# Attention slots in twos beside the mixer's channel steps, a planner with measured durations, and some weight sums on VectorE

## The chip, the core and the metric

The kernel runs on one core of one Trainium2 chip. The metric is the device time of one execution in microseconds, the median of ten runs. Every time below is of a device execution or of its profile.

## The reference

Block-sparse attention (BigBird), and after it a Fourier mixing block with a two-layer channel network. Cut to what matters:

```python
# q, k, v: (4 batches, 8 heads, 768 positions, 64), float32
scores = scale * q @ k.T                       # 768 x 768 for each head
mask: blocks of 32; the neighbours, first and last block rows and columns,
      and 3 sampled blocks for each block row
attn = exp(where(mask, scores, -1e9) - max); attn /= sum(attn)
x = (attn @ v)                                 # heads side by side: (4, 768, 512)

mixed = real(fft(fft(x, axis=1), axis=2))      # positions, then features
u = x + mixed
un = (u - mean(u)) / sqrt(var(u) + 1e-6)       # over features
out = u + relu(un @ w_ch1) @ w_ch2             # 512 -> 2048 -> 512
```

## The kernel before

**Engines.** TensorE (PE) multiplies, ScalarE (ACT) takes exponentials and copies out of the accumulation banks (PSUM), VectorE (DVE) adds, multiplies and folds, GpSimd (POOL) adds weights up, SyncE (SP) issues DMAs. Each takes its instructions strictly in the order in which the program issues them, and waits on semaphores. That order is fixed when the kernel is built: the source is a program that issues instructions slot by slot, with the framework's scheduler off.

**Attention.** Heads are taken in pairs: four pairs a batch, 16 in all, numbered n. For each pair the 768 queries are cut in two halves, and the 768 keys in six chunks of 128. One (pair, half, chunk) is a *unit*; two units are a *slot*. So there are 6 slots to a pair (s = 0 to 5 within it), 24 to a batch and 96 in all. A half takes three slots. For each slot the program issues:
- `scores`: for each unit two concurrent products, of 64 rows each, into one of the two score buffers `s` (L565). In the first batch, and in the second until its mixer steps turn to the channels, a second product adds the mask from two small factors (L575, `by_pe`).
- `weigh`: ScalarE's exponential into one of four buffers `e` (L585); where TensorE hasn't added the mask, the exponential in place (L588) and VectorE's product with the mask, `e<-s,mask` (L590). From the second batch on it also has GpSimd add the weights of a half up, unit after unit in place, in `acc` (L602, two adds a unit).
- `values`, for the slot before: two concurrent products of 64 columns into `o` (L615); after a half is complete, `o` is copied out, and later transposed into the mixer's input x (`place`, L637).
- `total` (L695): the sums over the keys from `acc`. In the first batch `add_up` (L681) does this on TensorE instead.
- `turn` (tp, L498): transposes of q and k of the next pair, in halves, through the one bank with the tag "t". From the third batch on, VectorE transposes in blocks, and ScalarE puts q in order (`in_order`, L540).

**The weights.** During the first batch, 32 chunks of the channel weights arrive by DMA in six rooms in turn, and ScalarE and VectorE round them (`w_round`, the last of five VectorE steps is L461). `keep_factors` (L478) copies the mask's two factors by two DMAs into room 2, after chunk 26 has been its last chunk, and from then on L575 reads the copy.

**The mixer.** While a batch's attention runs, the batch before goes through the mixer. Its first part stands in the queue `apart`: the scaling of rows (L723), folds of x on VectorE (`fold_0`, `fold_1`, `fold_e`, `fold_2`: L746 to L774), transforms on TensorE (zp, side, pq), arrival, normalisation on VectorE with a power on GpSimd (`spread`, L886), and transposes (utp). When it is through, its last step `go` puts the second part in the queue `late`: `quad`s (xp, yp, z: L1010, seven products each, which use both score buffers too) and channel steps y (L1066). Short steps (`place`, `total`, `turn`) wait in the queue `short`.

**The planner.** What is issued when between the slots is decided by estimates: `when` holds for each engine the time up to which it is planned to be busy, `busy(engine, us, after)` moves it on, and `free` holds when banks come free. `gap` issues a step of `apart` or `short` if its inputs and bank are planned to be ready. `state["owed"]` paces `late`, so that channel steps are spread over the slots of a batch.

The order of one slot before, as the source has it:

```python
for u, ps in scores(units): weigh(u, ps)
if not late: gap(1.5)
for u in done: values(u)          # the slot before
...                               # loads, short steps, channel steps
w_loads(); w_steps(sl)
if sl == SB - 3: keep_factors()   # SB = 24
```

Of the kernel before, what the change touches and what calls it, by code (L numbers as in the profile page):

```python
# [17 lines left out]
ALU = mybir.AluOpType  # L18
# [84 lines left out]
def kernel(  # L103
# [14 lines left out]
    nc = tc.nc  # L118
# [88 lines left out]

    pairs = [(b, j) for b in range(B) for j in range(NP)]
    loaded, v_of = {}, {}


    BY_VECTOR = 2 * NP + 1
# [269 lines left out]
    s_at, e_at, oT_at, acc_at = {}, {}, {}, {}  # L482

    def turn(n, a, half):

        t = loaded[n, a]
        if half == 0:
# [3 lines left out]
        tag, pool = ("m", ps_m) if first and a == 0 else ("t", ps_t)  # L491
        tp, at = pool.tile([P, 512], FP32, tag=tag, name="tp"), bank(tag)
        if a == 0:
            parts = [t[:, c // 2, c % 2, :, :] for c in (range(4, 6) if half else range(4))]
        else:
            parts = [t[:, T * half + c, :, :] for c in range(T)]
        for c, part in enumerate(parts):
            nc.tensor.transpose(tp[:, c * P:(c + 1) * P], part, ident)  # L498
        done = busy("PE", 0.15 * len(parts)) + HOP
        if a == 1:  # L500
            nc.scalar.copy(out=dst[:, half * HS:(half + 1) * HS], in_=tp[:, 0:HS])
            give(at, busy("ACT", 0.5, done))
        else:
            for i, (to, to_jump, frm, jump, cnt, step) in enumerate(_TURNED[half]):
                on, copy = (("DVE", nc.vector.tensor_copy) if n == 0 and half == 1
                            else ("ACT", nc.scalar.copy))
                copy(out=_grid(dst, to, 2, to_jump, cnt, 1),
                     in_=_grid(tp, frm, 2, jump, cnt, step))
                end = busy(on, 0.27 if cnt > 1 else 0.18, done)
            give(at, end)  # L510
        if half == 1:
# [67 lines left out]
    def weigh(u, s):  # L579
        n, w = divmod(u, UP)  # L580
        half, c = divmod(w, C)
        e = ep.tile([P, 2, HS], FP32, tag="e", name="e")
        e_of[u] = e
        if u in by_pe:
            nc.scalar.activation(out=e, in_=s[:, :, 0:HS], func=ACT.Exp, scale=scale)  # L585
            e_at[u] = busy("ACT", 0.8, s_at[u]) + HOP
        else:
            nc.scalar.activation(out=s[:, :, 0:HS], in_=s[:, :, 0:HS], func=ACT.Exp, scale=scale)  # L588
            m = mask[:, c, half * HS:(half + 1) * HS].rearrange("p (o s) -> p o s", o=1)
            nc.vector.tensor_tensor(out=e, in0=s[:, :, 0:HS], in1=m.broadcast_to([P, 2, HS]),  # L590
                                    op=ALU.mult)
            e_at[u] = busy("DVE", 0.97, busy("ACT", 0.8, s_at[u]) + HOP) + HOP
        if n < NP:
            return
        if c > 0:
            acc_at[n, half] = busy("POOL", 2.0, e_at[u]) + HOP
        if c == 1:
            acc_of[n, half] = acc_p.tile([P, 2, HS], FP32, tag="acc", name="acc")

        for i in range(2 if c > 0 else 0):  # L600
            acc = acc_of[n, half][:, i, :]
            nc.gpsimd.tensor_add(out=acc, in0=e_of[u - 1][:, i, :] if c == 1 else acc,  # L602
                                 in1=e[:, i, :])

    def values(u):
        n, w = divmod(u, UP)
        half, c = divmod(w, C)
        e = e_of[u]
        busy("PE", 0.75, e_at[u])
        vt = v_of[n]  # L610
        if c == 0:
            o_of[n, half] = ps_o.tile([P, HS], FP32, tag="o", name="o")
        o = o_of[n, half]
        for i in range(2):
            nc.tensor.matmul(o[D * i:D * i + D, :], vt[:, i, c, :], e[:, i, :],  # L615
                             start=(c == 0), stop=(c == C - 1))
# [118 lines left out]
    def fourier(b, xA, xB, uns):  # L735
# [163 lines left out]
                                    scalar2=rstd, op0=ALU.subtract, op1=ALU.mult)  # L899

        def d(us, fn, *args):
            return "d", lambda: fn(*args), 0.0, 0.0, us
# [302 lines left out]
    SP = UP // SLOT  # L1205
    SB = SP * NP
    W_PACE = 1.42
    short, apart, late = deque(), deque(), deque()
    state = {"w": 0, "got": 0, "owed": 0.0, "ready": 0.0}

    def channel_step():
        late.popleft()[0]()

    def do_apart():
        kind, fn, pe, act, dve, _ = apart.popleft()
        if kind in "dw":
# [12 lines left out]
        if kind != "-":  # L1229
            give(at, done - HOP)  # L1230
        state["ready"] = done

    def gap(rest=0.0, ahead=None, kinds="tm"):
# [4 lines left out]
        while apart:  # L1238
            kind, fn, pe, act, dve, need = apart[0]
            if len(late) > need:  # L1240
                break
            if kind in "dw":
# [26 lines left out]
    def begin(b):  # L1269
# [10 lines left out]
            factors["at"] = None  # L1280
        apart.append(("-", go, 0.0, 0.0, 0.0, hold))

    def w_loads():
# [9 lines left out]
    def slot(sl):  # L1293
        phase, r = divmod(sl, SB)
        n, s = divmod(sl, SP)
        units = range(SLOT * sl, SLOT * sl + SLOT)
        if sl < B * SB:
            for u, ps in scores(units):
                weigh(u, ps)
        if not late:  # L1300
            gap(1.5)
        if 0 < sl <= B * SB:
            done = [u - SLOT for u in units]
            for u in done:
                values(u)
            if phase == 0 or sl == SB:
                add_up(done)
            for u in done:
                e_of.pop(u)
        if s == 3 and n + 2 < len(pairs):  # L1310
# [5 lines left out]
        if sl > 0 and s == (5 if reuse else 3) and sl <= B * SB:  # L1316
            b, j = pairs[n]
            at = oT_at[n, 0]
            if reuse:
# [17 lines left out]
            short.append(("t", at, lambda: place(n - 1, 1)))  # L1337
        if sl > SB and s == 0 and sl <= B * SB:
            short.append(("t", acc_at[n - 1, 1], lambda: total(n - 1)))
        if n + 1 < len(pairs):  # L1340
            for at, a, half in ((1, 0, 0), (2 if n > 0 else 3, 0, 1), (4, 1, 0), (5, 1, 1)):
                if s == at and n + 1 < BY_VECTOR:
                    short.append(("t", 0.0, lambda a=a, half=half: turn(n + 1, a, half)))
            if s == 1:
                load_v(n + 1)
        if sl == 0:
# [5 lines left out]
        if r == 1 and 0 < phase:  # L1352
# [5 lines left out]
        gap(max(state["owed"], 0.0))  # L1358
        while late and state["owed"] >= late[0][1] / 2:
            state["owed"] -= late[0][1]  # L1360
            channel_step()
            gap(max(state["owed"], 0.0))

        while short and (s in (2, 5) or len(short) > 1 or phase == 0 or r == 0):
            ready = [i for i in short if max(i[1], min(free[i[0]])) <= when["PE"] + 0.1]
            if not ready and s not in (2, 5) and r > 0 and sl > 1:
                break
            item = ready[0] if ready else short[0]
            short.remove(item)
# [153 lines left out]
```

## Time and profile before

| | |
|---|---|
| median of 10 runs | 1090.04 us (1087.92 to 1092.57) |
| the profiled execution | 1087.79 us, its span 1086.1 us |
| granted TensorE clock, mean | 0.994 |
| ScalarE busy | 378.9 us, 35% of the span |
| slot 24 (second batch) begins | 129.84 us |
| slot 48 (third batch) begins | 294.06 us |
| slot 72 (fourth batch) begins | 557.16 us |
| last scores (slot 95) begin | 799.62 us |
| the chain that ended last | TensorE 90%, VectorE 5%, ScalarE 2% |
| GpSimd's adds (L602), two a unit | 192 at 1076 ns and 48 at 1061 ns on the mean |

Rows of the timeline have the start in us from the span's beginning, the time from there to the end of the group, engine, line, operation, what is written and read, the shapes, the number of instructions, and in brackets the idle time of the engine ahead of it and what ended it. Instructions of TensorE overlap, so the spacing of starts tells what they cost. A float32 product is two passes, and so two instructions in the trace (x8 of s are two units). In the rows of windows follow the stretch, its length, then busy time and instructions of TensorE, its weight loads, VectorE, ScalarE and GpSimd, then the granted clock, the DMA share and GB/s. The rows of a tile give least, median and greatest duration in ns, first and last start, and shapes.

### The profile page before, as it was taken

Reading aid. Unit: us, or ns where it says so; the run is one execution under the profiler, and the core shown is the slowest. Engines: PE = TensorE matmul, PEld = TensorE weight load, DVE = VectorE, ACT = ScalarE, POOL = GpSimd, SP = SyncE. Lnnn points to the kernel's source line nnn. Section 1 sums busy time; section 2 is a strip of 40 time slices with the busy share of each in tenths; the row PEclk is TensorE's granted clock in tenths of the full one; section 3 lists DMA queues with packets and bytes.
Section 4 is the critical chain, followed back from the end, with each engine's and each line's share of the span. In section 5 each row is a group of like instructions: output and inputs, shape, how many; then the busy total and the mean of one; then the engine's idle time right before and its main releaser. Section 6 shows DMA issues by size and latency. Waiting matters only on the chain.

```text
span 1086.1 us, 12509 instructions
## 1 busy us (share of the span) xinstructions
PE 1052.1 (97%) x4410; PEld 536.9 (49%) x4410; DVE 648.4 (60%) x1203; ACT 378.9 (35%) x762; POOL 274.1 (25%) x302
## 2 busy tenths in 40 slices
PE   8999889999999999999999999999999999999996
PEld 4434335454444555443444555443344555568575
DVE  5899783554468265665577446555557355675663
ACT  5888655552331212344342302334320202220210
POOL 1000094852343001355455000344630001000000
PEclk9999899999999999999999999999999999999998
DMA  7757311110110001223211000212000001000001
GB/s 223 219 175 238 97 31 30 44 30 15 19 25 1 1 1 33 55 40 56 43 21 32 1 0 15 64 33 40 12 8 7 1 0 30 30 1 0 1 19 44
DMA packets 108483, 47.07 MB, mean 43 GB/s; under 512 B 95854, under 2 KB 101244, under 8 KB 108412
## 3 DMA queue, kind: packets, MB, share of 16 engines
q1 hardware_dynamic: 106524, 45.38, 16.3%
q10 hardware_dynamic: 1856, 0.79, 0.3%
q8 instruction: 37, 0.61, 0.2%
q14 instruction: 34, 0.28, 0.1%
q0 software_dynamic: 32, 0.01, 0.0%
HBM read 37.11 MB, written 6.29 MB: 40 GB/s over the span
## 4 chain that ended last, share of the span: by engine, by line
PE 90%; DVE 5%; ACT 2%; issue 1%; DMA 1%; POOL 0%; SPq 0%; POOLq 0%; ACTq 0%; DVEq 0%
PE y L1066 23%; PE z L1010 15%; PE s L565 11%; PE o L615 11%; PE yp L1010 8%; PE yy L1129 6%; PE xp L1010 4%; PE zp L823 2%; PE tp L498 1%; PE sp L681 1%; PE s L575 1%; PE utp L935 1%; PE sp L695 1%; PE zp L794 1%; PE xt L637 1%
## 5 line engine op out<-in xcount | busy, mean ns | idle before, releaser
L602 POOL TENSOR_TENSOR acc<-acc,e 128x384 f32<-128x384 f32 x192 | 200.3, 1076 | 127.5 <-DVE e L590 118.0
L565 PE MATMUL s<-qT,kT 64*128 64x384 f32 x768 | 153.6, 515 | 5.2 <-DVE e L590 3.8
L615 PE MATMUL o<-e,vr 128*64 128x384 f32 x768 | 146.4, 503 | 0.0
L1069 DVE TENSOR_TENSOR x<-y,x 128x512 f32<-128x512 f32 x72 | 49.7, 690 | 147.7 <-PE y L1066 147.7
L1066 PE MATMUL y<-w_sb,hA 128*128 128x512 f32 x288 | 131.1, 598 | 1.7 <-ACT zs L825 1.7
L1066 PE MATMUL y<-w_sb,hB 128*128 128x512 f32 x288 | 129.0, 597 | 0.7 <-DVE x L1069 0.7
L590 DVE TENSOR_TENSOR e<-s,mask 128x768 f32<-128x768 f32 x106 | 96.3, 949 | 45.2 <-ACT s L588 43.0
L588 ACT ACTIVATE s<-s 128x768 f32<-128x768 f32 x106 | 80.3, 789 | 116.6 <-PE s L565 116.0
L602 POOL TENSOR_TENSOR acc<-e 128x384 f32<-128x384 f32 x48 | 49.9, 1061 | 234.7 <-ACT e L585 129.9
L565 PEld LDWEIGHTS s<-qT,kT 64*128 64x128 f32 x768 | 63.5, 185 | 80.0 <-issue 23.0
L1010 PE MATMUL z<-unT,t 128*128 128x384 f32 x256 | 93.0, 486 | 0.0
L1015 DVE TENSOR_TENSOR hA<-z,hA 128x384 f32<-128x384 f32 x64 | 35.7, 558 | 89.5 <-PE z L1010 88.7
L1066 PEld LDWEIGHTS y<-w_sb,hB 128*128 128x128 f32 x288 | 53.2, 190 | 67.6 <-issue 65.6
L1066 PEld LDWEIGHTS y<-w_sb,hA 128*128 128x128 f32 x288 | 52.4, 190 | 65.7 <-issue 58.5
L615 PEld LDWEIGHTS o<-e,vr 128*64 128x64 f32 x768 | 46.8, 137 | 74.7 <-issue 70.1
L886 POOL TENSOR_SCALAR st<-st 128x1 f32<-128x1 f32 x24 | 6.7, 279 | 280.6 <-DVE st L885 280.2
L585 ACT ACTIVATE e<-s 128x768 f32<-128x768 f32 x86 | 65.1, 813 | 27.5 <-PE s L575 26.1
L1019 ACT ACTIVATE hA<-hA 128x384 f32<-128x384 f32 x64 | 33.5, 523 | 117.8 <-DVE hA L1015 117.4
L1010 PEld LDWEIGHTS z<-unT,t 128*128 128x128 f32 x256 | 48.6, 190 | 33.9
L1019 ACT ACTIVATE hB<-hB 128x384 f32<-128x384 f32 x64 | 33.5, 523 | 86.4 <-DVE hB L1015 86.4
L1010 PE MATMUL xp<-unT,w_sb 128*128 128x384 f32 x128 | 47.7, 495 | 0.3 <-DVE x L1069 0.3
L1010 PE MATMUL yp<-unT,w_sb 128*128 128x384 f32 x128 | 46.9, 489 | 0.5 <-DVE un L859 0.5
(202 smaller groups left out, 1387.9 us busy)
## 6 DMA issues: line engine op xcount, KB each, us to landing
wraw<-in_moe_w_ch_dram SPq DMA_DIRECT2D x32, 512.0 KB
vr<-in_v_dram SPq DMA_DIRECT2D x30, 192.0 KB
qr<-in_q_dram SPq DMA_DIRECT2D x48, 64.0 KB
x<-oT SPq DMA_DIRECT2D x192, 12.0 KB
kr<-in_k_dram SPq DMA_DIRECT2D x14, 192.0 KB
qb<-in_q_dram SPq DMA_DIRECT2D x28, 96.0 KB
kb<-in_k_dram SPq DMA_DIRECT2D x28, 96.0 KB
out_dram<-x SPq DMA_DIRECT2D x16, 128.0 KB
```

Of the source, the lines that this page charges most:

```text
L565: nc.tensor.matmul(s[:, i, 0:HS], kT[rows, c * P:(c + 1) * P], qT[rows, queries], start=True, stop=u not in by_pe)
L585: nc.scalar.activation(out=e, in_=s[:, :, 0:HS], func=ACT.Exp, scale=scale)
L588: nc.scalar.activation(out=s[:, :, 0:HS], in_=s[:, :, 0:HS], func=ACT.Exp, scale=scale)
L590: nc.vector.tensor_tensor(out=e, in0=s[:, :, 0:HS], in1=m.broadcast_to([P, 2, HS]), op=ALU.mult)
L602: nc.gpsimd.tensor_add(out=acc, in0=e_of[u - 1][:, i, :] if c == 1 else acc, in1=e[:, i, :])
L615: nc.tensor.matmul(o[D * i:D * i + D, :], vt[:, i, c, :], e[:, i, :], start=(c == 0), stop=(c == C - 1))
L1010: nc.tensor.matmul(to, a[:, k, :], c[:, k, :], start=(k == 0), stop=(k == ND // 2 - 1))
L1015: tt(out=to, in0=ps, in1=a, op=ALU.add)
L1019: nc.scalar.activation(out=h, in_=h, func=ACT.Relu)
L1066: nc.tensor.matmul(y, hs[0, half][:, l, m * P:(m + 1) * P], w2_sb[:, 4 * r + l, :], start=(l == 0), stop=(l == 3))
L1069: nc.vector.tensor_tensor(out=x[:, m, :], in0=y, in1=x[:, m, :], op=ALU.add)
L1129: nc.tensor.matmul(ps, a[:, k, :], c[k // 2][:, k % 2, :] if isinstance(c, list) else c[:, k, :], start=(k == 0), stop=(k == 3))
```

## The change

1. *Slots in twos.* From the first even slot with channel steps in `late`, two slots are issued together: scores of the even slot, values of the two slots before, scores of the odd slot, and channel and short steps only after that. Where the first of the two waiting slots ends a half, its values come ahead of the even slot's scores. Values thus run up to two slots behind (the queue `due`).
2. *Planned durations.* A GpSimd sum is put down at 2.9 us instead of 2.0. A fold is planned 0.75 us longer for each of its instructions while GpSimd is planned to be busy. The planner also tracks when a buffer `e` is free again (`e_free`).
3. *Sums.* In the second batch, where TensorE adds the mask, the sum of a unit is issued after its values, and VectorE does it, in one add of 128 x 768, if it is planned to be done sooner than GpSimd would be. As built, 19 units go to VectorE, and GpSimd keeps 202 of its 240 adds.
4. *Banks and places.* From the pair n = 5 on, the second half of q is transposed through a bank with the tag "m" instead of "t". `keep_factors` runs in slot 19 instead of 21. `total` is issued by s = 1 at the latest. Loads of q, `place` and the mixer's beginning follow the new place of the values; other short steps may wait longer, and all are forced at s = 3 and 5 once slots are paired.

Cut to its core:

```diff
+    def turn_on(n, a, half):
+        return "m" if n > NP and (a, half) == (0, 1) else "t"
...
-            e_at[u] = busy("ACT", 0.8, s_at[u]) + HOP
+            e_at[u] = busy("ACT", 0.8, max(s_at[u], e_free.pop(u - 2 * SLOT, 0.0))) + HOP
...
-        if n < NP:
-            return
-        if c > 0:
-            acc_at[n, half] = busy("POOL", 2.0, e_at[u]) + HOP
...
+            if n >= NP:
+                gather(u)
+
+    def gather(u):
+        n, w = divmod(u, UP)
+        half, c = divmod(w, C)
+        if c == 0:
+            return
...
+        at = max(e_at[u], acc_at.get((n, half), 0.0))
+        if u in by_pe and factors["at"] and max(when["DVE"], at) + 1.0 < max(when["POOL"], at) + 2.9:
+            nc.vector.tensor_tensor(out=acc, in0=start, in1=e, op=ALU.add)
+            acc_at[n, half] = busy("DVE", 1.0, at) + HOP
+        else:
+            for i in range(2):
+                nc.gpsimd.tensor_add(out=acc[:, i, :], in0=start[:, i, :], in1=e[:, i, :])
+            acc_at[n, half] = busy("POOL", 2.9, at) + HOP
+        e_free[u] = acc_at[n, half]
...
+        if u in by_pe and n >= NP:        # in values(u), after its products
+            gather(u)
...
+        OPS = {fold_0: 1, fold_1: 1, fold_e: 3, fold_2: 2}
+    def behind(kind):
+        at = max(when["DVE"], state["ready"])
+        return 0.75 * (len(kind) - 1) if when["POOL"] > at else 0.0
...
-        if sl < B * SB:
-            for u, ps in scores(units):
-                weigh(u, ps)
-        if not late:
-            gap(1.5)
-        if 0 < sl <= B * SB:
-            done = [u - SLOT for u in units]
...
+        opens = sl % 2 == 0
+        state["paired"] |= opens and len(late) > 0
+        paired = state["paired"]
...
+        if paired and len(due) == 2 and due[0] % SP % T == T - 1:
+            sum_up()
+        got = scores(units) if sl < B * SB else ()
+        if paired and len(due) == 2:
+            sum_up()
+        for u, ps in got:
+            weigh(u, ps)
+        if not paired and not late:
+            gap(1.5)
+        while due and (opens or not paired):
+            sum_up()
+        due.append(sl)
...
+        more = paired and opens and sl < B * SB
+        if not more:
+            gap(rest())
+        while not more and rest():
             state["owed"] -= late[0][1]
             channel_step()
+            gap(rest())
...
-        if sl == SB - 3:
+        if sl == SB - 5:
             keep_factors()
```

`sum_up` takes the first slot of `due`, and issues `values` for its units (and in the first batch `add_up`). Nothing in the order after the last attention slot changes but that its last values come two slots at a time.

More of the change, by code (lines that the diff above doesn't have):

```diff
@@ L481 @@
     turned, e_of, acc_of, o_of, sums_of, x_of, sp_of = {}, {}, {}, {}, {}, {}, {}
-    s_at, e_at, oT_at, acc_at = {}, {}, {}, {}
+    s_at, e_at, e_free, oT_at, acc_at = {}, {}, {}, {}, {}
+    def turn_on(n, a, half):
+        return "m" if n > NP and (a, half) == (0, 1) else "t"
     def turn(n, a, half):
         t = loaded[n, a]
-        if half == 0:
+        first_of = (n, a) not in turned
+        if first_of:
             turned[n, a] = tp_p.tile([P, S], FP32, tag="qk"[a] + "T", name="qk"[a] + "T")
@@ L490, in turn @@
         first = n == 0 and half == 0
-        tag, pool = ("m", ps_m) if first and a == 0 else ("t", ps_t)
+        tag, pool = ("m", ps_m) if first and a == 0 or turn_on(n, a, half) == "m" else ("t", ps_t)
         tp, at = pool.tile([P, 512], FP32, tag=tag, name="tp"), bank(tag)
@@ L510, in turn @@
             give(at, end)
-        if half == 1:
+        if not first_of:
             flat = t.rearrange("p t r i d -> p (t r i d)" if a == 0 else "p c i d -> p (c i d)")
@@ L592, in weigh @@
             e_at[u] = busy("DVE", 0.97, busy("ACT", 0.8, s_at[u]) + HOP) + HOP
-        if n < NP:
+            if n >= NP:
[4 more added lines that the diff above has]
+        if c == 0:
             return
-        if c > 0:
-            acc_at[n, half] = busy("POOL", 2.0, e_at[u]) + HOP
         if c == 1:
             acc_of[n, half] = acc_p.tile([P, 2, HS], FP32, tag="acc", name="acc")
[L600 to L603, printed above, removed]
+        acc, e = acc_of[n, half], e_of[u]
+        start = e_of[u - 1] if c == 1 else acc
+        at = max(e_at[u], acc_at.get((n, half), 0.0))
[7 more added lines that the diff above has]
+        e_free[u] = acc_at[n, half]
     def values(u):
@@ L901, in d @@
         def d(us, fn, *args):
[L902 removed]
+            return "d" + "d" * OPS.get(fn, 0), lambda: fn(*args), 0.0, 0.0, us
+        OPS = {fold_0: 1, fold_1: 1, fold_e: 3, fold_2: 2}
         first = [d(1.8, fold_0, 0), d(1.8, fold_0, 1), d(1.0, fold_1, 0), d(0.9, fold_e),
@@ L1207 @@
     W_PACE = 1.42
-    short, apart, late = deque(), deque(), deque()
-    state = {"w": 0, "got": 0, "owed": 0.0, "ready": 0.0}
+    short, apart, late, due = deque(), deque(), deque(), deque()
+    asked = set()
+    needed = set()
+    state = {"paired": False, "total": None, "w": 0, "got": 0, "owed": 0.0, "ready": 0.0}
     def channel_step():
         late.popleft()[0]()
+    def behind(kind):
+        at = max(when["DVE"], state["ready"])
+        return 0.75 * (len(kind) - 1) if when["POOL"] > at else 0.0
     def do_apart():
         kind, fn, pe, act, dve, _ = apart.popleft()
-        if kind in "dw":
+        if kind[0] in "dw":
+            dve += behind(kind)
             state["ready"] = busy("DVE", dve, rstd_at[0] if kind == "w" else state["ready"]) + HOP
@@ L1241, in gap @@
                 break
-            if kind in "dw":
+            if kind[0] in "dw":
+                dve += behind(kind)
                 if kind == "w" and rstd_at[0] > max(when["DVE"], when["PE"]) + 0.2:
@@ L1281, in begin, with rest, once @@
         apart.append(("-", go, 0.0, 0.0, 0.0, hold))
+    def rest():
+        return state["owed"] if late and state["owed"] >= late[0][1] / 2 else 0.0
+    def once(*of):
+        if of in asked:
+            return False
+        asked.add(of)
+        return True
     def w_loads():
@@ L1296, in slot, with sum_up @@
         units = range(SLOT * sl, SLOT * sl + SLOT)
-        if sl < B * SB:
-            for u, ps in scores(units):
-                weigh(u, ps)
-        if not late:
-            gap(1.5)
-        if 0 < sl <= B * SB:
-            done = [u - SLOT for u in units]
+        opens = sl % 2 == 0
+        state["paired"] |= opens and len(late) > 0
+        paired = state["paired"]
+        def sum_up():
+            at = due.popleft()
+            done = range(SLOT * at, SLOT * at + SLOT)
             for u in done:
                 values(u)
-            if phase == 0 or sl == SB:
+            if at < SB:
                 add_up(done)
@@ L1309, in slot @@
                 e_of.pop(u)
-        if s == 3 and n + 2 < len(pairs):
+        if paired and len(due) == 2 and due[0] % SP % T == T - 1:
[10 more added lines that the diff above has]
+        due.append(sl)
+        if s >= (4 if paired else 3) and n + 2 < len(pairs) and (n + 2, 0) not in loaded:
             load_q(n + 2)
@@ L1315, in slot @@
         reuse = n % NP == 0 and phase >= 2
-        if sl > 0 and s == (5 if reuse else 3) and sl <= B * SB:
+        if s >= (5 if reuse else 3) and (n, 0) in oT_at and once(n):
             b, j = pairs[n]
@@ L1339, in slot @@
             short.append(("t", acc_at[n - 1, 1], lambda: total(n - 1)))
+            state["total"] = short[-1]
+        if r == 0:
+            needed.clear()
+            needed.update(map(id, short))
         if n + 1 < len(pairs):
-            for at, a, half in ((1, 0, 0), (2 if n > 0 else 3, 0, 1), (4, 1, 0), (5, 1, 1)):
-                if s == at and n + 1 < BY_VECTOR:
-                    short.append(("t", 0.0, lambda a=a, half=half: turn(n + 1, a, half)))
+            for at, a, half in ((1, 0, 0), (2 if n > 0 else 3, 0, 1),
+                                (3 if paired else 4, 1, 0), (5, 1, 1)):
+                if s >= at and n + 1 < BY_VECTOR and once(n + 1, a, half):
+                    short.append((turn_on(n + 1, a, half), 0.0,
+                                  lambda a=a, half=half: turn(n + 1, a, half)))
             if s == 1:
@@ L1351, in slot @@
             short.append(("m", 0.0, lambda: mask_step(sl - 4)))
-        if r == 1 and 0 < phase:
+        if r > 0 and 0 < phase and not needed.intersection(map(id, short)) and once("mixing", phase):
             begin(phase - 1)
@@ L1357, in slot @@
         state["owed"] = min(state["owed"], pace) + pace if late else 0.0
-        gap(max(state["owed"], 0.0))
-        while late and state["owed"] >= late[0][1] / 2:
+        more = paired and opens and sl < B * SB
+        if not more:
+            gap(rest())
+        while not more and rest():
             state["owed"] -= late[0][1]
             channel_step()
-            gap(max(state["owed"], 0.0))
-        while short and (s in (2, 5) or len(short) > 1 or phase == 0 or r == 0):
+            gap(rest())
+        must = (3, 5) if paired else (2, 5)
+        soon = r == 0 and all(i[1] < when["PE"] + 1.0 for i in short)
+        if s == 1 and state["total"] in short:
+            short.remove(state["total"])
+            state["total"][2]()
+        while short and (not more or soon) and (
+                s in must or len(short) > 1 or phase == 0 or soon or sl == B * SB):
             ready = [i for i in short if max(i[1], min(free[i[0]])) <= when["PE"] + 0.1]
-            if not ready and s not in (2, 5) and r > 0 and sl > 1:
+            if not ready and s not in must and 1 < sl < B * SB and not soon:
                 break
```

## The prediction

> **What bounds the kernel now.** I read four views in this order. First the page's busy times: TensorE is busy for 97% of the span, and no other engine comes near.
>
> ```profile
> PE 1052.1 (97%) x4410; PEld 536.9 (49%) x4410; DVE 648.4 (60%) x1203; ACT 378.9 (35%) x762; POOL 274.1 (25%) x302
> ```
>
> So a gain has to be TensorE's own work or one of its few waits. The second view, who waited for whom on TensorE, names them (total, times, longest):
>
> ```profile
> PE s L565 <- DVE e L590: 3.8, 3, 1.7
> PE zp L794 <- DVE sa L767: 3.7, 1, 3.7
> PE tp L498 <- ACT qT L507: 3.4, 3, 1.1
> PE s L575 <- DMA factors<-at_q: 3.3, 1, 3.3
> ```
>
> The third is the timeline, for the price of a change of array shape. Scores use 64 rows (s, L565), values 64 columns (o, L615), the mixer the whole array:
>
> ```profile
> 466.81 1.56 PE L565 MATMUL s<-qT,kT 64*128 64x384 f32 x8
> 468.30 1.51 PE L615 MATMUL o<-e,vr 128*64 128x384 f32 x8
> 469.74 1.56 PE L1010 MATMUL xp<-unT,w_sb 128*128 128x384 f32 x4
> 471.13 1.45 PE L1010 MATMUL yp<-unT,w_sb 128*128 128x384 f32 x4
> 472.42 1.45 PE L1010 MATMUL z<-t,w_sb 128*128 128x384 f32 x4
> ```
>
> Read the starts. yp to z is 1.29 us for four passes of 384 columns with no change of shape. xp, the first after o, takes 1.39; o, changed on both sides, 1.44; s 1.49. The last pass before a change costs 0.10, the first after it 0.10, or 0.05 for o. A change therefore costs 0.15 to 0.20 us.
>
> The fourth is the timeline around the moved copy of the mask factors:
>
> ```profile
> 106.69 0.49 PE L575 MATMUL s<-at_q,at_k 64*128 64x384 bf16 x4
> 110.56 0.69 DVE L461 TENSOR_TENSOR w_sb<-w_sb,wraw 128x512 f32<-128x512 f32 x1
> 111.16 3.82 SPq L252 DMA_DIRECT2D qr<-in_q_dram  x6
> 115.08 0.55 SPq L478 DMA_DIRECT2D factors<-at_k  x1
> 115.68 0.60 SPq L478 DMA_DIRECT2D factors<-at_q  x1
> 119.07 0.82 PE L575 MATMUL s<-factors 64*128 64x384 bf16 x4 [3.27 <-DMA factors<-at_q]
> ```
>
> 106.69 is the mask step of slot 20, 119.07 that of slot 22. L461 at 110.56 is the last step of weight chunk 26, the last user of the room that the factors are copied into.
>
> **Part by part**, against the profiled execution (1087.79 us, span 1086.1; the median of the runs is 2.25 higher).
>
> *Slots in twos.* s, o, channels, s, o, channels becomes s, o, o, s, channels. In the built order of TensorE's instructions shape changes go from 350 to 319. By kind most of those lost are o to full array (39), scores to o (26) and full array to scores (21); 25 o to scores and 22 scores to full array are new. 31 fewer at 0.15 to 0.20 is 4.6 to 6.2; kind by kind with the edges above, **-5.0**. All of it is on the path. Does the pair bring a wait? The second s needs the score banks that VectorE's mask product reads: from the starts at 463.66 (s), 464.62 (exp) and 465.52 (two products, 1.82) the first product ends 2.8 us after its s began. The pair gives it 1.49 + 2.71 = 4.2 us, and at the end of a half (o, s, o, s) 2.9, as back-to-back slots have now at 0.12 each. In one place only (slot 73 to 74) just 1.95 us stands between two scores: **+1.0**.
>
> *More mask products on TensorE.* The first batch's channels start three slots later, so slots 43 and 44 add their mask by matmul: two runs at 0.32, **+0.6**.
>
> *ScalarE's reordering copy (L540, 1.86).* At 461.11 and 715.37 it holds up the exponentials, and the next scores wait (1.73 each in the timeline, with edges 1.8). Paired, it is issued between the exponentials of both slots: those of the first end 2.5 us after its s, the copy then ends at 4.4, and the second slot's exponential starts at 4.2 + 0.96 = 5.2. **-3.6.**
>
> *Factors copied two slots earlier.* The order of SyncE puts the copies ahead of the six q loads, but also has slots 20 and 21 read the copy. It cannot start before chunk 26 ends, 110.56 + 0.69 = 111.25, and nothing ahead of that differs. From issue to use took 119.07 - 115.08 = 4.0 us, so slot 20's mask step can start at 115.25, not at 106.69: a wait of **8.6**. Slot 22's present wait (its scores start at 114.19, would end at 115.6, and the mask step comes at 119.07) is 3.4. Net **+5.1**; if two copies without q loads beside them land in 2 us, +3.2. Behind the wait stand o and sp of slot 19 on TensorE; slot 20's exponentials and behind these the ScalarE steps of chunks 27 and 28. The q loads move from 111.16 to about 112.5 for a use near 141. After the 3.4 us wait the clock was halved:
>
> ```profile
> 119.00:125.00 6.00, 5.93 (x24) 1.76 (x24) 3.72 (x8) 1.89 (x3) 0.00 (x0) 0.52 0.00 0
> ```
>
> PEclk is 0.52 there, and TensorE's work took 2.4 us longer. I charge the same once more: no change. [...]
>
> *Second q half in the other bank.* Where six transposes share one bank, the second two wait for ScalarE's six copies: 1.28 with edges, at 142 and 209. Both go, **-2.6**. One k pair (slot 41) now stands without an o between: ScalarE's 0.48 copy and the hops, **+0.6**.
>
> *VectorE adds weights.* 19 of the 35 sums in which TensorE adds the mask go to VectorE: one 128x768 add each, nearest row L590 (same size, from PSUM), 949 ns; 38 GpSimd adds (median about 1.0, longest 2.5) go. TensorE waits for neither, but for the folds (1st batch, from 148 us), which GpSimd's adds slow down:
>
> ```profile
> L750 DVE TENSOR_TENSOR sa<-sa x4: 949/950/1749, 152.8 to 832.2; 128x765 f32<-128x765 f32 x4
> L767 DVE TENSOR_TENSOR sa<-sa x4: 550/551/1345, 159.4 to 836.1; 128x384 f32<-128x384 f32 x4
> ```
>
> Least and greatest are the same instruction without and with GpSimd adding beside it: 0.8 us each. Now zp waits 3.7 for sa and 0.9 (with edges) for e: 4.6. Afterwards zp stands one slot later: TensorE arrives at 157.06 + 5.1 - 1.28 + 3.25 = 164.1. The row scaling ahead of the folds (6.25) loses contention in four of six (1.04 to 0.69, the row of L1069): -1.4; one add, +1.0; so folds start at 147.96 + 5.1 - 0.4 = 152.7. sa was ready 12.7 later; two of the slowed folds then run after GpSimd has finished (-1.6): 163.8. No wait for sa, none for e. But the total (sp) now stands right behind zp, and needs the add queued behind the last fold: about 0.8. So **-3.8**; with contention as now the waits are 2.6 + 1.1 + 1.9 = 5.6, that is +1.0. [...]
>
> The other adds go in order: behind an add that waits for GpSimd's previous one stand evictions of the mixer and totals. No row shows such a wait. Below, a gain is excluded: between 164 and 250 us TensorE has no wait to lose but the one at 209. Above, one GpSimd sum (two adds at 11.61 / 8 = 1.45, so 2.9) in two places makes 5.8. I take **+1.0**, near the lower end, since VectorE is busy for only 45.0 of those 86 us.
>
> Sum: -5.0 + 1.0 + 0.6 - 3.6 + 5.1 - 2.6 + 0.6 - 3.8 + 1.0 = **-6.7**. The profiled time becomes 1081.1, the median 1090.0 - 6.7 = **1083.3**.
>
> **Rivals.** *The folds stay as late as now* (contention merely changes sides): waits at zp and sp of 5.6, -6.7 + 4.8 = -1.9, 1088.1. [...] Against: GpSimd keeps only 7 of the 10 sums of the pair of heads that runs there. *VectorE's queue blocks*: its adds wait for GpSimd's in the same sum, in slots 26 to 44, and folds and whitening behind them go late. From 6.7 us of added waits on, the change is slower: two sums of 2.9 waited for (5.8) in place of my 1.0, and the waits at zp and sp kept (4.8), give -6.7 + 4.8 + 4.8 = +2.9, 1092.9. For it: VectorE takes its instructions in order, and the sums alternate between the two engines. Against: only one such add stands between the row scaling and the folds, and GpSimd's part of its sum should be done some 3 us earlier. *The copy lands early or the wait is hidden*: -1.9 more, and no add loss, 1080.4. That pairing does not happen is excluded by the order.
>
> **How the numbers follow.** Forecast 0.50, folds as late 0.22, queue blocked 0.16, copy early 0.12. A measurement here tells 0.2%, 2.2 us, from no change. Faster takes the forecast, the early copy and a third of "folds as late" (0.69), same the rest of that (0.15), slower the blocked queue (0.16). The range reaches from 1079, the early copy with changes at 0.20, to 1092, just short of the blocked queue's centre.
>
> **What would show it.** TensorE's wait for the factors should read some 8 us near 107 to 115 with the half clock behind it; tp on qT only once; s on e gone near 461; zp on sa below 1; the third of these failing means folds, an acc on VectorE waiting on GpSimd means the queue. I'm wrong if slot 24 starts less than 3 us late, or if the second scores of a pair wait over 0.5 us throughout.

## The result, and the profile after

The changed kernel takes 1083.09 us (median of 18 runs, 1082.10 to 1084.07), the kernel before 1088.05 (62 runs, 1085.07 to 1092.57): ratio 0.995, 95% interval 0.9942 to 0.9959. The kernel before thus ran 2 us faster over many runs than in the ten of the opening table. The profiled execution took 1084.00 us, span 1082.2, against 1087.79 and 1086.1: 3.8 us less. So there are two figures for the gain, 3.8 between the two profiled runs and 5.0 between the medians; experiments 1 to 4 bear on why they differ.

The page's busy times:

```profile
PE 1047.1 (97%) x4418; PEld 540.9 (50%) x4418; DVE 657.1 (61%) x1218; ACT 377.9 (35%) x762; POOL 236.5 (22%) x264
```

TensorE still bounds, with 5.0 us less busy time. VectorE has gained 15 instructions, and GpSimd lost 38. Who waited for whom on TensorE (total, times, longest):

```profile
PE s L580 <- DMA factors<-at_q: 8.8, 1, 8.8
...
PE xp L1033 <- DVE x L1092: 2.6, 3, 1.8
PE s L570 <- DVE e L595: 2.2, 2, 1.3
...
PE tp L503 <- ACT qT L512: 1.1, 1, 1.1
...
PE zp L814 <- DVE sa L787: 0.9, 1, 0.9
PE xt L657 <- DVE sums L685: 0.8, 1, 0.8
...
PE tp L503 <- ACT kT L506: 0.6, 1, 0.6
```

The wait for the factors has grown from 3.3 to 8.8. The one for sa fell from 3.7 to 0.9, and two of the three for qT are gone. The one of scores for the mask products (s on e) fell from 3.8 in three places to 2.2 in two, and neither of the two is at the old places. xp waiting for x (1.8 in one place), xt for sums and tp for kT are not among the four that were read before. The timeline around the moved copy, SP's queue and the score products:

```profile
104.99 1.56 PE L570 MATMUL s<-qT,kT 64*128 64x384 f32 x8
...
111.02 0.53 SPq L479 DMA_DIRECT2D factors<-at_k  x1
111.60 0.59 SPq L479 DMA_DIRECT2D factors<-at_q  x1
115.34 0.82 PE L580 MATMUL s<-factors 64*128 64x384 bf16 x4 [8.79 <-DMA factors<-at_q]
```

The copy starts at 111.02, where chunk 26 lets it, and is used 4.3 us later, now by slot 20, whose scores begin at 104.99 (`L580` is the mask product that stood at L575 before). The clock behind it, by windows (start:end, length, busy times of PE, PEld, DVE, ACT and POOL, granted TensorE clock, DMA share, GB/s):

```profile
108.00:114.70 6.70, 0.00 (x0) 0.00 (x0) 2.82 (x5) 0.00 (x0) 0.00 (x0) 0.69 0.66 214
114.70:121.00 6.30, 5.66 (x24) 1.63 (x26) 0.00 (x0) 1.55 (x3) 0.00 (x0) 0.52 0.00 2
```

It is halved during the wait already, and TensorE works at half clock until 120.7. The row scaling ahead of the folds in the first batch (least, median, greatest ns; first and last start), and the chain behind it up to zp and the total (sp):

```profile
L743 DVE TENSOR_TENSOR x<-x,r x6: 679/681/1480, 146.7 to 150.6; 128x512 f32<-128x512 f32 x6
```
```profile
152.10 2.55 DVE L766 TENSOR_TENSOR sa<-x 128x1536 f32<-128x1536 f32 x1
...
155.46 9.09 POOL L619 TENSOR_TENSOR acc<-acc,e 128x384 f32<-128x384 f32 x6
157.04 1.75 DVE L770 TENSOR_TENSOR sa<-sa 128x765 f32<-128x765 f32 x1
...
163.62 1.35 DVE L787 TENSOR_TENSOR sa<-sa 128x384 f32<-128x384 f32 x1
165.00 0.56 DVE L788 TENSOR_TENSOR sa<-sa 128x384 f32<-128x384 f32 x1
165.02 0.94 PEld L814 LDWEIGHTS zp<-cs_sb,sa 128*128 128x128 f32 x4 [1.32 <-DVE sa L787]
...
167.13 0.95 DVE L614 TENSOR_TENSOR acc<-acc,e 128x768 f32<-128x768 f32 x1
168.14 0.14 PEld L715 LDWEIGHTS sp<-acc,pick 128*32 128x32 f32 x4 [0.83 <-DVE acc L614]
```

Four of the six scalings run at 680 ns, without GpSimd beside them. The folds run beside GpSimd as before, up to and with the first of L787 (1.35 against 0.55); only what comes after 164.55, where GpSimd's adds end, is undisturbed. The total then waits 0.83 for VectorE's add of weights (L614) that is queued behind the folds.

### The profile page after: what moved, and what is told of

Read it like the earlier page. It is cut to its first block, busy times and chain, and to the rows that moved or that the text cites. A ratio compares the mean times of both kernels' runs of the same rounds, so it can differ in the third digit from the quotient of the medians.

```text
span 1082.2 us, 12497 instructions
## 1 busy us (share of the span) xinstructions
PE 1047.1 (97%) x4418; PEld 540.9 (50%) x4418; DVE 657.1 (61%) x1218; ACT 377.9 (35%) x762; POOL 236.5 (22%) x264
## 4 chain that ended last, share of the span: by engine, by line
PE 90%; DVE 6%; ACT 1%; issue 1%; DMA 0%; POOL 0%; SPq 0%; ACTq 0%; POOLq 0%; DVEq 0%
PE y L1089 23%; PE z L1033 15%; PE s L570 12%; PE o L633 11%; PE yp L1033 8%; PE yy L1152 6%; PE xp L1033 4%; PE zp L843 2%; PE sp L701 1%; PE tp L503 1%; PE s L580 1%; PE zp L814 1%; PE utp L958 1%; PE sp L715 1%; PE xt L657 1%
## 5 line engine op out<-in xcount | busy, mean ns | idle before, releaser
L619 POOL TENSOR_TENSOR acc<-acc,e 128x384 f32<-128x384 f32 x162 | 165.6, 1058 | 232.4 <-ACT e L590 142.4
L633 PE MATMUL o<-e,vr 128*64 128x384 f32 x768 | 142.6, 500 | 0.0
L595 DVE TENSOR_TENSOR e<-s,mask 128x768 f32<-128x768 f32 x102 | 92.8, 951 | 56.6 <-ACT s L593 49.3
L593 ACT ACTIVATE s<-s 128x768 f32<-128x768 f32 x102 | 77.5, 792 | 98.3 <-PE s L570 97.9
L590 ACT ACTIVATE e<-s 128x768 f32<-128x768 f32 x90 | 68.5, 816 | 39.4 <-PE s L580 33.8
L619 POOL TENSOR_TENSOR acc<-e 128x384 f32<-128x384 f32 x40 | 44.9, 1142 | 109.6 <-PE sp L715 92.5
```

What stands on the lines that cost most here:

```text
L619: nc.gpsimd.tensor_add(out=acc[:, i, :], in0=start[:, i, :], in1=e[:, i, :])
```

## The experiments

They ran on three chips, each beside the kernel before, and ratios are to that; its median was 1087.01 (experiments 1, 2, 6 and 7), 1089.2 (4, 5, 8 and 10) and 1087.24 (3 and 9). Nothing is issued in another order ahead of slot 0, and yet it starts between 7.83 and 9.67 us in the 14 profiles: a difference of two spans can be off by as much as 1.8 us, and where it matters, the starts of slots are given too. Below, a *gap* is the distance between two starts on TensorE less the price of the work between them, edges included, as in the prediction.

### 1. The copy of the factors late again

The changed kernel with one line as before:

```
-        if sl == SB - 5:
+        if sl == SB - 3:
             keep_factors()
```

> The changed kernel with one thing undone: the factors are copied in slot 21 again, not in slot 19. My theory: the move costs what the prediction put down, a wait of 8.6 us in slot 20 in place of one of 3.4 in slot 22, so undoing it gives back 5.1 us: 1078 us, with slot 24 beginning near 129.8 us of the span. Rival, that the wait is made up later because VectorE's rounding and folds go on meanwhile: no difference from the changed kernel (1083), slot 24 early but the second batch's waits longer by as much.

Measured: 1076.64, ratio 0.9903 (0.9884 to 0.9922), span 1074.4, TensorE's wait for the factors 3.5. The early copy alone cost 5 us by ratio and 7.8 by span (from slot 20 to slot 24 29.91 us in the changed kernel, 22.14 here). In the profile the clock makes 7.8 out of the expected 5.1:

```profile
112.00:119.00 7.00, 3.12 (x22) 0.96 (x20) 6.69 (x17) 3.88 (x7) 0.00 (x0) 1.00 0.53 161
119.00:125.00 6.00, 6.00 (x44) 2.50 (x41) 4.06 (x9) 4.30 (x8) 0.00 (x0) 1.00 0.00 0
```

Here the clock stays at 1.00 after a gap of 3.75. In the profile of before it was halved after a gap of 3.49 (0.52 in the row 119.00:125.00 that the prediction shows). That the clock also parts 5 from 7.8 is not shown. The ratio is uncertain by 2 us, and the mean clocks of the other five runs (0.995 and 0.996, against 0.998 in the profiled one) point to half clock in most of them, though four of the five took only 0.4 to 0.6 us longer.

### 2. The copy at slot 22, ahead of the q loads

```
+        if sl == SB - 3:
+            keep_factors()
         if s >= (4 if paired else 3) and n + 2 < len(pairs) and (n + 2, 0) not in loaded:
             load_q(n + 2)
...
-        if sl == SB - 5:
-            keep_factors()
```

> The changed kernel with the factors copied in slot 21, but issued ahead of the six q loads of that slot. If the copies only wait for weight chunk 26 (done at 111.25 us) and for their place in SyncE's queue, they start near 111.3 and have landed by 115.3, when slot 22's scores end at about 115.6: no wait for the factors, and no stretch of half clock behind it. That is 8.8 + 2.4 = 11.2 us less than the changed kernel, 1072 us. Rival, that ScalarE or VectorE then holds TensorE up at the same place, since they are behind with the rounding: only the 5.1 us of copying late, 1078.

Measured: 1072.29, ratio 0.986 (0.9839 to 0.9882), span 1070.6. As expected, the wait is gone:

```profile
110.78 0.53 SPq L479 DMA_DIRECT2D factors<-at_k  x1
111.36 0.59 SPq L479 DMA_DIRECT2D factors<-at_q  x1
112.06 5.04 SPq L253 DMA_DIRECT2D qr<-in_q_dram  x6
113.62 1.62 PE L570 MATMUL s<-qT,kT 64*128 64x384 f32 x8 [0.35 <-ACT e L590]
115.10 0.50 PE L580 MATMUL s<-factors 64*128 64x384 bf16 x4
```

Slots 20 and 21 read the uncopied factors, the copy has 3.7 us from its second DMA until slot 22's mask step (just enough: in experiment 10 that step waits 0.45), and the q loads leave one us later than in before. The clock is at 1.00 throughout this stretch.

### 3. Before, without the wait for the factors

The same move in the kernel before, and nothing else; the order on the other four engines is unchanged.

> Before, with one change: the copies of the factors are issued in slot 22 ahead of that slot's q loads, so that the mask step finds them. Theory: the wait of 3.5 us in before is near the length at which the clock is halved or not, from run to run, and this is what spreads its times from 1085 to 1092.6. Without the wait: 3.5 less for it and 2.4 less for the half clock of the profiled run, 1081.9, ratio 0.993 to 0.995, TensorE's granted clock at 1.00 between 110 and 130 us, and times within some 1.5 us of each other. Rival: the spread has another source; then the times still lie over 4 us apart.

Measured: 1082.89, ratio 0.9961 (0.9944 to 0.9978), span 1081.2. The gap falls to 0.31 and the clock there is 1.00, but the times still lie 5.5 us apart (1081.09 to 1086.59): the expected narrow spread did not come. The trace names a second place. TensorE's wait for the folds, a gap of 3.73 here as in before, is followed by half clock in this run and was not in the profile of before. Windows around its end, before first (zp starts at 160.76), then this run (at 153.4):

```profile
160.00:164.00 4.00, 2.53 (x10) 1.42 (x12) 3.90 (x6) 0.01 (x1) 2.83 (x3) 1.00 0.00 0
164.00:168.00 4.00, 4.00 (x24) 1.90 (x24) 0.44 (x2) 1.80 (x5) 0.00 (x0) 1.00 0.32 102
```
```profile
152.20:159.20 7.00, 5.76 (x18) 3.04 (x19) 4.82 (x7) 1.39 (x4) 3.31 (x3) 0.76 0.05 12
```

A third one lies behind the gap of 1.81 at 709, where scores wait for exponentials held up by the reordering copy: half clock from 712.7 to 716.1, 1.8 us lost; in before there is none behind the same gap at 715. So the kernel before has two waits of 3.5 to 3.7 us and two of 1.8, and two of the four, the one of 3.73 and the one of 1.81 at 715, came with half clock in one of the two profiles and without it in the other. The granted clock of the twelve runs and their times go together: 0.995 to 0.996 in those of 1081.1 to 1082.7, 0.994 from 1082.8 to 1083.2, 0.990 to 0.991 from 1085.8 to 1086.6. The rival (another source) is not supported; the theory was right in kind and had missed three of four such waits.

### 4. The pairs alone

Of the change only slots in twos and their rules (and the tracking of `e`); GpSimd adds every sum, issued in `weigh` and planned at 2.0, and the rest is as before:

```
-        return "m" if n > NP and (a, half) == (0, 1) else "t"
+        return "t"
...
-        if u in by_pe and factors["at"] and max(when["DVE"], at) + 1.0 < max(when["POOL"], at) + 2.9:
+        if False:
...
-        OPS = {fold_0: 1, fold_1: 1, fold_e: 3, fold_2: 2}
+        OPS = {}
...
-        if sl == SB - 5:
+        if sl == SB - 3:
```

> The pairs alone: of the change only the order of the slots in twos and its rules are kept; every add of weights is GpSimd's and is issued with its exponential, the old durations are back, the factors are copied at slot 22, and the second q half is turned in the bank of the others. By the prediction's terms against before: -5.1 of TensorE's own work by the built order (its 0.6 for two mask products inside), -3.6 for the reordering copy, +1.0 at slot 73 to 74: -7.7, ratio 0.993. If the unforeseen waits of the changed kernel (1.4 near 290 us, 2.0 near 697, 0.9 near 279) come from the pairs and not from VectorE's adds, they come here too: -3.4, 0.997. Rival: the waits make up for all of the gain, ratio 1.000 or above.

Measured: 1085.73 (1081.57 to 1088.16), ratio 0.9964 (0.9945 to 0.9983), span 1082.8: -3.9 by ratio, -3.3 by span (0.6 of it ahead of slot 0), near the value with the unforeseen waits. And they are here:

```profile
PE xp L1031 <- DVE x L1090: 4.0, 3, 1.8
PE s L580 <- DMA factors<-at_q: 3.8, 1, 3.8
PE zp L812 <- DVE sa L785: 3.7, 1, 3.7
PE tp L503 <- ACT qT L512: 3.4, 3, 1.1
...
PE z L1031 <- DVE hA L1036: 1.9, 1, 1.9
```

The gaps are 1.99 at 447 and again at 698 (xp), 2.11 at 306 (z) and 0.92 at 297. They come without any VectorE add of weights. The range is wide, as before's; in the profiled run both waits of 3.7 to 4.1 were followed by half clock.

### 5. The rules around the pairs, without pairs

As experiment 4, with `state["paired"] = False`.

> As the pairs alone, but with the flag for pairs kept false, so that only the changed rules around the pairs are left (when a transposition, a total or a q load may be issued). If the rules cost nothing by themselves, the time is that of before, ratio 0.998 to 1.002. If the 24 us that the changed kernel lost without its pairs came from these rules (the placement issued before its output buffer was stored, with exponentials queued behind it), the ratio is 1.010 or more here too, with ScalarE's x copy waiting some 7 us for a store near 711 us.

Measured: 1088.3, ratio 0.9993 (0.9976 to 1.0009), span 1088.0. The rules cost nothing that shows (the interval is some 2 us to either side), and the two gaps of 1.81 in front of scores (461 and 716 us, where ScalarE reorders) are there again; so it is the pairs that took them away.

### 6. The changed kernel without pairs

```
-        state["paired"] |= opens and len(late) > 0
+        state["paired"] = False
```

> The changed kernel with slots never paired. Its order has 29 more shape changes, 4.4 us by the edges' prices, and ScalarE's reordering copy holds up the exponentials again at two places, 3.6 us: 8.0 us longer, less 1.0 for the pair of scores that stood too close at slot 74: 1090 us. Rival, that pairing gives nothing because each pair waits for its score buffers: the time stays at 1083 with fewer waits of s for e.

Measured: 1114.05, ratio 1.0244 (1.0222 to 1.0267), 24 us more than expected, and no price of pairing. One place shows why. ScalarE's timeline near 711 us:

```profile
711.45 0.48 ACT L658 COPY x<-xt 128x384 f32<-128x384 f32 x1 [6.99 <-DMA out_dram<-x]
711.82 1.88 ACT L545 COPY qT<-qb 128x256 f32<-128x256 f32 x6
713.61 1.49 ACT L593 ACTIVATE s<-s 128x768 f32<-128x768 f32 x2
```

ScalarE stands 7 us before a copy into an x buffer that the output DMA still reads, and the next exponentials are queued behind it. TensorE then waits 4.7 us at 712, 3.4 at 726 and 5.2 at 757, and behind each the clock is halved for 6.8 us:

```profile
707.00:764.00 57.00, 42.16 (x190) 16.53 (x188) 36.77 (x44) 24.73 (x45) 35.99 (x39) 0.82 0.19 36
```

So 14.8 us of idle time and three spells of half clock stand in these 57 us. Experiment 5 has the same rules and no such stall, so it takes the other parts' timing too; which of them is open, as is what remains of the 24 us.

### 7. No adds of weights on VectorE

The changed kernel, all sums on GpSimd and issued in `weigh` (`if False:` in place of the comparison, and no call of `gather` in `values`); the measured durations stay.

> The changed kernel with all sums on GpSimd (240 adds, none on VectorE), issued with the exponential. If the sums on VectorE speed the folds up, as predicted, waits at zp of some 3 to 5 us come back near 165 us of the span, and the time is about 4.8 us longer, 1088. Rival, that contention just changes sides: within 1 us of the changed kernel, and the waits at zp stay below 1.5 us because the planner now plans folds longer. Its order has 3 more shape changes, and 2 us more of TensorE work by the edges' prices.

Measured: 1088.56, ratio 1.002 (1.0006 to 1.0034), span 1086.4. By span that is 4.2 more than the changed kernel, by ratio 7.6, where 4.8 was expected. The place is not the expected one: zp waits for nothing. The scaling runs beside GpSimd again:

```profile
L741 DVE TENSOR_TENSOR x<-x,r x6: 828/1482/1493, 144.9 to 151.3; 128x512 f32<-128x512 f32 x6
```

It takes 7.87 us instead of 4.58, but the planner, which knows the longer folds, puts zp at 171.2 and other work ahead of it. The loss turned up elsewhere: the total's product sp behind ScalarE's x (a gap of 2.27 at 164), scores behind a mask product (2.04 at 432), and 1.9 us more work by the built order. So the contention is back as expected, but that it costs what the prediction put down is not shown here, since the order moved with it.

### 8. The old durations

The changed kernel with `OPS = {}` and 2.0 for GpSimd's sum in both places.

> The changed kernel with the scheduler's old durations (a GpSimd sum 2.0, no surcharge on folds beside GpSimd). If the durations are what puts folds, zp and VectorE's adds into places where nothing waits, then zp waits some 4 us for the folds again, or the total as long: ratio to before 0.998. If they change nothing that TensorE waits for: 0.994 to 0.995, as the changed kernel.

Measured: 1091.65, ratio 1.0028 (1.0013 to 1.0042), span 1089.7: 7.5 us behind the changed kernel by span, more than expected, and slower than before. The planner now brings TensorE to zp at 161.4, and the folds, with GpSimd beside them, are done at 166.6:

```profile
166.63 0.50 PEld L814 LDWEIGHTS zp<-cs_sb,sa 128*128 128x128 f32 x2 [5.83 <-DVE sa L787]
```

After that gap of 5.24 the clock is halved for 6.8 us (four gaps of 0.3 to 0.7 in the work that follows, 2.0 together), and two gaps of some 2 us stand at 246 and 305.

### 9. Pairs and bank, without the wait for the factors

Three kernels build on experiment 3. The bank alone, then the pairs alone (as in experiment 4), then both:

```
-        tag, pool = ("m", ps_m) if first and a == 0 else ("t", ps_t)
+        tag, pool = ("m", ps_m) if first and a == 0 or (n > NP and (a, half) == (0, 1)) else ("t", ps_t)
```

> The run before in this list (before, without the factor wait) plus the second q half of the later pairs in the mixer's bank. By the prediction -2.6 against it: 1079.3, the two waits of 1.28 of tp on qT gone and the one near 16 us left. Rival: the mixer's bank is busy there and the channels wait for it instead, no difference.

Measured: 1082.44, ratio 0.9945 (0.9926 to 0.9965), span 1081.1: by median 0.45 and by span 0.1 less than experiment 3, not 2.6 (from slot 0 on 1.3 less). Two of the three waits of tp went, and the one of zp grew:

```profile
PE zp L794 <- DVE sa L767: 5.2, 1, 5.2
...
PE tp L498 <- ACT qT L507: 1.1, 1, 1.1
```

The folds did not stay where they were. In experiment 3 (first row) the row scaling ahead of them took 6.24 us, and here (second row) 7.88, since all of it runs beside GpSimd's adds:

```profile
134.35 6.24 DVE L723 TENSOR_TENSOR x<-x,r 128x512 f32<-128x512 f32 x6
```
```profile
135.42 7.88 DVE L723 TENSOR_TENSOR x<-x,r 128x512 f32<-128x512 f32 x6
```

Both begin 11.83 us after slot 24 (122.52 and 123.59), so the folds end 1.6 later, while TensorE comes to zp at the same time, 27.3 and 27.4 after slot 24: the 1.3 that it saved went into an o that now stands ahead of zp. It waited 1.5 longer. Behind it came 6.8 us of half clock (3.4 in experiment 3), and gaps of 0.89 and 0.73 at 192 and 218.

> Before without the factor wait, plus the pairs and their rules alone. By the prediction's terms -7.7 against the first run of this list; with the waits that the pairs brought in the run of the pairs alone (2.1 near 306 us, 2.0 near 447 and near 698, 0.9 near 297), -2.9: 1079.0. Rival (the prediction's terms as they stood): 1074.2.

Measured: 1078.39, ratio 0.9909 (0.9887 to 0.9931), span 1076.7: 4.5 less than experiment 3 by median and by span (4.1 from slot 0 on); half clock took about as much in both profiles (2.7 here, 1.3 and 1.8 there). Between the two expected values, nearer to the one with the waits.

> Before without the factor wait, plus pairs and bank. What parts it from the changed kernel with the factors ahead of the q loads (1072.3, ratio 0.986) is only VectorE's adds of weights and the measured durations. If these are worth some 4 us, this takes 1076 to 1077, ratio 0.990. If pairs and bank have already taken what there was: 1072 to 1073, 0.986.

Measured: 1081.73, ratio 0.9935 (0.9911 to 0.9959), span 1080.4. Neither expected value came: the bank made the pairs 3.3 us slower by median and 3.7 by span, of which 1.4 lie ahead of slot 0. Against experiment 2 (span 1070.6), from which only VectorE's adds and the durations part it, 9.8 are missing: 6.0 of them between slots 30 and 34, where zp waits 5.24 instead of 1.0 and half clock follows, and 3.4 between slots 34 and 72, where half clock follows a gap of 2.11 too (some 1.7 of the 3.4).

### 10. The fastest version

Experiment 2, with the second halves of q and k in the mixer's bank for all later pairs:

```
-        return "m" if n > NP and (a, half) == (0, 1) else "t"
+        return "m" if (n > NP and half == 1) or (n, a, half) == (1, 0, 1) else "t"
```

> The changed kernel with the factors copied at slot 22 ahead of that slot's q loads, and second halves of q and k turned in the mixer's bank for every pair but those of the start. Against the run with the factors ahead of the q loads alone (ratio 0.986): -1.3 for the wait of tp on qT that is left near 17 us and -0.6 for the one of tp on kT near 222, so 1070.4 on a chip on which before takes 1087.0, ratio 0.984. Rival: the mixer's bank is held by the mask or the channels there, and the ratio stays at 0.986.

Measured: 1071.17, ratio 0.9836 (0.9814 to 0.9857), span 1070.2 against 1070.6. The gap of 0.73 at kT fell to 0.31; the wait near 16 us, of which I expected 1.3, is still there (`PE tp L503 <- ACT qT L512` reads 1.1 once), since it belongs to another half than the one I moved. It beats the kernel before by 1.6% and the changed one by 1.1%, and the latter is nearly all the copy's place.

## Why the prediction was right, and where not

The total was right: 6.7 us forecast as the gain, 3.8 between the profiled runs, 5.0 between the medians. 1083.3 lies so near to 1083.09 partly by luck: the median of before over more runs was 2 us below the one I started from, and the gain was 1.7 to 2.9 us smaller than forecast. Most of what was missed are the last two terms below.

- **Slots in twos and mask products (-5.0, +0.6).** Unchanged by what was measured: TensorE's work by the built orders falls by 4.4, and its busy time by 5.0. Experiments 4 and 9 show a gain of 3.3 to 4.5 after all waits that pairs bring.
- **The reordering copy (-3.6), slot 73 to 74 (+1.0), the k pair (+0.6).** Right: both gaps of 1.81 are gone, the new ones are 0.90 and 0.73. (The copy starts at 459.98 and 714.23 in before; the times that the prediction gives are not its starts.)
- **The factors (+5.1).** Right in size and mechanism: the gap grew from 3.49 to 8.96, slot 24 starts at 134.90 and not 129.84, and half clock took about as much in both profiles: 2.6 us in before, where I had 2.4 (from slot 22's mask step to slot 24 10.77, against 8.13 in experiment 3), 2.5 in the changed kernel (from slot 20's mask step to slot 22 9.99, against 7.49 in experiment 1). What I had not seen is that a wait of 3.5 us need not be followed by half clock: after the gap of 3.75 in experiment 1 the clock stayed at 1.00.
- **The bank (-2.6).** The two waits are gone in the changed kernel, but as a term of its own it is wrong: experiment 9 shows next to nothing gained where zp still waits for the folds, since the order and the folds move with it. What it is worth together with the next one, in which I had let TensorE arrive 1.28 sooner, no run shows by itself.
- **VectorE's adds and folds (-3.8).** The waits at zp and sp went from 4.6 to 1.97: -2.6. TensorE arrived when I had said (164.08), and the total waits for VectorE's add as long as I had said (0.83). The step that failed is "two of the slowed folds then run after GpSimd has finished (-1.6)". GpSimd adds until 164.55, L770 takes 1.75 and the first L787 1.35 as before, and from the first fold to the end of the last one needed it takes 12.9 us (152.10 to 165.0), against 12.8 before. What shortened the wait is that four of the six scalings ran without GpSimd, not two (4.58 instead of 6.25, 1.7 where I had 1.4), and that TensorE comes to zp later than in before. That folds beside GpSimd's adds are slowed showed again (1.35 against 0.55). By span the changed kernel loses 4.2 without the adds (experiment 7) and 7.5 without the durations (experiment 8), and experiment 2 loses 9.8 without both (experiment 9): both do something, the durations more, but the half clock behind some of the gaps is in these figures.
- **Other adds (+1.0).** Apart from the total's, counted above, no wait of TensorE could be traced to an add of weights on VectorE, and the last of these adds starts at 231.9 us. Instead, all behind it, gaps of 1.99 (697), 1.40 (290), 0.92 (279), 0.56 (447) and 0.33 (247) came, 5.2 in all, and gaps at other places went or shrank, by 1.7 in all (680, 783 and 311 us in before). Experiment 4, with every sum on GpSimd, has the gaps of 1.99 (698) and 0.92 (297) too, and others of 1.99 (447) and 2.11 (306): these are the pairs' price, which I had put at one place. The 1.40 at 290 is not among them. There a mask product is queued behind row scalings that take 1.48 beside GpSimd's adds, and which part of the change brings that is not shown. Mis-sized by 2.5 us in all (3.5 where I had 1.0). At 697 VectorE's queue shows how:

```profile
695.38 1.48 DVE L995 TENSOR_TENSOR unT<-unT 128x512 f32<-128x512 f32 x1
...
696.28 3.79 POOL L619 TENSOR_TENSOR acc<-acc,e 128x384 f32<-128x384 f32 x3
696.79 1.48 DVE L995 TENSOR_TENSOR t<-unT,t 128x512 f32<-128x512 f32 x1
...
698.66 0.68 DVE L1092 TENSOR_TENSOR x<-y,x 128x512 f32<-128x512 f32 x1
```

The subtractions for the channels' products (L995), 0.68 alone, take 1.48 beside GpSimd's adds, and x, for which xp waits, is behind them.

By terms: -4.4 - 3.6 + 5.3 - 2.6 + 0.7 + 0.9 - 2.6 + 5.2 - 1.7 = -2.8 (the factors as the change of all gaps between 104 and 130 us, 6.77 to 12.08). The other -1.0 to the 3.8 measured is left over for gaps of under 0.5, 0.3 of it ahead of slot 0; it was not traced further.

**The rivals.** "The folds stay as late" described the chain rightly and its effect wrongly, since TensorE arrived later too. "VectorE's queue blocks" came true in one sense only, by contention and with no add in it. "Copy early" is out: the copy took 4.3 us from issue to use with no q loads beside it. (Not alone, though: the row 108.00:114.70 has the DMA moving 214 GB/s. How long the copy takes by itself no run shows.)

**Why the medians part by more.** A wait of 9 us came with 10.2 us of half clock in all four profiles that have one (the changed kernel and experiments 6, 7 and 8), and of other gaps over 1.5 us behind its start the changed kernel has one (697 us), with no half clock behind it in the profile; the 18 runs of its median lie within 2 us. Before has four, of 3.7, 3.5, 1.8 and 1.8, and a range of 7.5; its profiled run, with the clock halved behind one of them, lay 0.3 under the median. This is argued from the spreads and clocks of experiments 1 to 4 and 9; no run changed the clock alone.

## What to carry to other kernels

A short wait on TensorE was not priced by its length: those of 1.8 to 4 us cost up to 2.9 us more behind them or nothing more (next section), so take them away altogether, and look at them first where run times spread. Where a copy is late, move it ahead of the bulk transfer in front of it on its queue before moving it to an earlier consumer: one place in SyncE's order was worth 4.35 us here, in before (experiment 3) as in the changed kernel (2 against 1), and two slots earlier cost 5 to 8. And a gain ahead of a wait can be lost in it: the bank's 1.3 us brought TensorE to zp no sooner, and the folds ended 1.6 later (experiment 9). So the wait has to go first, and an estimator that places the waiting step has to know the contended durations.

## What the runs showed of the hardware

In the 14 profiles the clock was halved for 3.4 us at gaps of 4.07, 3.84, 3.73, 2.11, 2.04 and twice 1.81, for 6.8 at gaps of 3.49, 3.71, twice 3.73, twice 5.24, 5.25 and the three waits of experiment 6, and for 10.2 at gaps of 8.96, 9.15, 9.27 and 9.32 (the spell that begins behind TensorE's last product is left aside). At gaps of 3.75 (experiment 1), 3.73 (zp in the profile of before), 2.27 (experiment 7) and both of 1.81 in before it was not.

So below 4 us a gap's length did not tell whether the clock was halved, nor for how long: gaps of 3.73 came with none, with 3.4 us and with 6.8. Before has two outcomes in one profile. The wait for the factors (a gap of 3.49) has the clock at 0.52 from 119.00 to 125.00, in the row that the prediction shows; the wait for the folds (3.73) has it at 1.00 in both rows of experiment 3. What decided between them is not shown here. What a spell took, as gaps in the work behind it, was 1.3 to 1.8 us for 3.4 and 2.0 to 2.9 for 6.8 in the profiles.
